# Transposes by halves of the array's rows in a second pass, and value weights cast ahead of the rows in an opening

## The chip, the cores and the metric

The kernel runs on one core of a Trainium2 chip. The metric is the device time of one execution in microseconds (us); smaller is better. TensorE is called PE here (PEld is its weight load), VectorE DVE, ScalarE ACT, GpSimd POOL, and the engine that only issues DMAs SP. SBUF is the memory from which the engines read; PSUM is where PE writes its results.

## The reference

Four residual layers, A, B, A, B, on 2048 rows of 512 numbers, with 32 heads of 16 columns:

```
x = x + A(layernorm(x)); x = x + B(layernorm(x))      # twice
A: q, k, v = x @ wqkv, by heads;  pq = q @ w_phi[h];  pk = k @ w_phi[h]
   phi(p) = [softmax(p), softmax(-p)]                  # 32 features
   o = phi(pq) @ (phi(pk)^T v) / (phi(pq) . sum phi(pk) + 1e-6);  return o @ wo
B: per segment of 512 rows: softmax attention inside it, gated with
   a read of a memory that sums phi(k)^T v over the earlier segments; @ wo
```

Layer A is linear in the rows: a first pass over all rows sums the state phi(pk)^T v, a second pass reads it for each row. These are the linear layers of the change.

## The kernel before, in words

Everything is computed to about fp32 accuracy: each operand of a large product is split into a high part (the fp32 number rounded to a shorter format, "fp32r", by a cast on ACT) and a low part (a subtraction on DVE or POOL), and a product is three products: high by high, high by low, low by high. `mm3` writes these for the four blocks kc of the 512 inner numbers, block by block; with `low_last` it first takes those whose moving rows or columns are high. All PE instructions are issued through `mm` (L177) and `tp` (L181, a transpose: a matmul with the identity as moving operand), and `held` keeps them in the order of the code. All other instructions go through a helper at L155, which keeps the order of the code on each engine; SP issues the DMAs in the order of the code too. In `out<-in` names the second name behind the comma of a PE row is the operand that is loaded into the array.

**Opening** (`LayerA.first`). SP asks for the key weights, the first 512 rows and the value weights. While the rows' layer norm is computed (`moments` to `refine`, `normal`: tags st and x), PE folds w_phi into the key weights. `columns` transposes one tile of 128 normalised rows (four transposes into a PSUM tile g), casts it (ACT: hh) and takes the low part (DVE: hl). Behind the four `columns` come the value weights' casts on ACT (w<-P) and their low parts, by turns on DVE and POOL; then `v_tile` computes the values of the four tiles of rows.

**Second pass** (`LayerA.pass2`), one step i for each of the 16 tiles of 128 rows. A tile's features e (tag P) are exponentials of the query projections tb, 1024 per row; `scale_q` sums them on DVE (es), takes reciprocals (rr) and scales half of them on POOL (P<-P,rr). `transposed` turns them by eight transposes into the PSUM tile lg, which ACT copies to phT (P<-lg). `products` multiplies phT, loaded by 64 columns, with the state KN (32 small products into two PSUM tiles g), and DVE divides (r, U). In the next step `turn` transposes the row of outputs U by four transposes into g; ACT casts it (oh), DVE takes the low part (ol), and `out_proj` multiplies it with the output weights w, whose eight loads (high and low part of each kc by turns) are asked for at the pass's start; DVE adds the residual rows (ot<-g,ot) and SP stores them. The features are turned one step ahead, and scaled two ahead. The pass is woven with layer B's opening by a table of step numbers. The last output tiles (from i = 12) and the transposes of tiles 14 and 15 are handed on to layer B, which takes them in slots chosen by a count of PE work (`work`). The PSUM tiles g have several buffers; lg, mx and my have one each.

Of the kernel before, what the change touches and what calls it, by code (L numbers as in the profile page):

```python
# [7 lines left out]
F32 = mybir.dt.float32  # L8
F32R = mybir.dt.float32r
# [92 lines left out]
def interleave_kernel(ctx, tc, x_in, a_wqkv, a_wphi, a_wo, b_wq, b_wk, b_wv, b_wo, b_beta,  # L102
# [76 lines left out]
    def tp(*a):  # L179
        work[0] += 108  # L180
        return held(nc.tensor.transpose(*a))  # L181

# [252 lines left out]
    def mm3(po, lhs, rhs, kcs=range(NC), low_last=False):  # L435

        terms = [(kc, a, b) for kc in kcs for a, b in ((0, 0), (0, 1), (1, 0))]
        if low_last:
            terms.sort(key=lambda x: x[1])
        for n, (kc, a, b) in enumerate(terms):  # L440
            mm(po, lhsT=lhs(a, kc), rhs=rhs(b, kc), start=(n == 0), stop=(n == len(terms) - 1))
            if n % 3 == 2 and n < len(terms) - 1:
                yield
# [33 lines left out]
    def tok_proj(po, hT, t, w):  # L477
        yield from mm3(po, lambda a, kc: hT[a][:, kc, t * P : (t + 1) * P], lambda b, kc: w[b][:, kc, :])

    def turn(ot):  # L480

        o = [T2("oh", OO, F32R), T2("ol", OO, F32R)]
        pt = PS("g", G)
        for c, block in enumerate(ot):
            tp(pt[:, c * P : (c + 1) * P], block, ident)
        pt, hi, lo = [t[:, 0 : len(ot) * P] for t in (pt, *o)]
        act.copy(hi, pt)
        wait(lambda: dve.tensor_tensor(out=lo, in0=pt, in1=hi.bitcast(F32), op=SUB))
        return o

# [52 lines left out]
    def v_tile(hT, w, vv, tag, order=range(4), pairs=False):  # L543
# [4 lines left out]
        if not pairs:  # L548
            for t in order:
                po = PS(*tag)  # L550
                yield from tok_proj(po, hT, t, w)
                act.copy(v[:, t, 0 : H * VW].rearrange("p (h e) -> p h e", e=VW)[:, :, 0:DH],
                         po.rearrange("p (h e) -> p h e", e=DH))
                yield
            return
# [94 lines left out]
    class LayerA:  # L650
# [4 lines left out]
        def first(self, hT, vv, upcoming):  # L655

            wph = T2("U", UU)[:, 0 : NC * DH].rearrange("p (c f) -> p c f", c=NC)
            act.dma_start(out=ident, in_=c_ident)
            act.dma_start(out=bd, in_=c_bd)
            act.dma_start(out=wph, in_=a_wphi.rearrange("(c h) d f -> (h d) c f", c=NC))  # L660
# [25 lines left out]
            next(kfold)  # L686
            normal(st, 0, xt[0])
# [3 lines left out]
            for t in range(4):  # L691
                columns(hT, t, xt[t])
            upc = upcoming(1)
            next(upc[1])
            for kc in range(NC):
                act.copy(vh[:, kc, :], vraw[kc])
                low(pool if kc % 2 else dve, wv, kc, vraw[kc])
            for kc in range(NC):
                act.copy(kh[:, kc, :], kf[kc])
                low(dve, wk, kc, kf[kc])  # L700
            vt = v_tile(hT, wv, vv, ("g", G))
# [230 lines left out]
        def transposed(self, i):  # L932
# [6 lines left out]
            for half in range(2):  # L939
                for q in range(4):  # L940
                    g = 4 * half + q
                    tp(pt[:, half, q * P : (q + 1) * P], ef[:, g * P : (g + 1) * P], ident)
                if i in (1, 2):
                    act.copy(f[:, 4 * half : 4 * half + 4].rearrange("p g t -> p (g t)"), pt[:, half])
                elif half == 1:
                    act.copy(f.rearrange("p g t -> p (g t)"), pt.rearrange("p h x -> p (h x)"))
# [18 lines left out]
        def pass2(self):  # L965
# [5 lines left out]
            for i in range(NT):  # L971
                soon = [i + 2] if i < NT - 5 else [i + 2, i + 3] if i == NT - 5 else [i + 3]
                soon = [n for n in soon if 2 < n < NT]
                if i > 0:
                    if i <= NT - 4:
                        oT = turn([self.o[:, c * P : (c + 1) * P] for c in range(NC)])
# [4 lines left out]
                    if i >= NT - 4:  # L981
                        yield from transposed(i + 1)
                    yield from self.products(i)
                if 2 < i < NT - 4:
                    yield from transposed(i + 1)
# [11 lines left out]
                if 0 < i <= NT - 4:  # L997
                    steps = out_proj(x, self.xdst, i - 1, oT, self.wo, i == 1)
# [634 lines left out]
```

## Time and profile before

| | |
|---|---|
| median of three runs | 1307.09 us (1305.85 to 1308.08) |
| the profiled execution | 1307.07 us, its span 1305.4 us |
| mean granted clock of PE | 0.999 |
| busy in the span | PE 97%, PEld 76%, DVE 82%, ACT 64%, POOL 58% |
| turning the features (lg<-ident,P) | 256 transposes, 35.9 us busy |
| turning the outputs (g<-ident,U) | 96 transposes, 14.4 us busy |
| reading the state (g<-KN,P) | 1024 products, 37.4 us busy |
| DMA | 196.59 MB in the span, 151 GB/s in the mean |

Busy times of PE overlap: a matmul's row runs from its issue to its end, and the next one starts before that. So the cost of one of a row of equal matmuls is read from start to start, not from its duration. In a timeline row the count behind x tells how many equal instructions follow each other; the time is from the first's start to the last's end. In brackets stands how long the engine was idle before, and which engine's work ended that (the releaser). Idle time of an engine that isn't waited for costs nothing.

### The profile page before, as it was taken

The numbers are of one execution on the slowest core, as the hardware profiler recorded it, in microseconds if no ns is written. First come the engines' busy times: TensorE is split into PE (matmuls) and PEld (weight loads), VectorE is DVE, ScalarE is ACT, GpSimd is POOL, SyncE is SP. The second block draws the span as 40 slices with busy tenths as digits, with TensorE's granted clock in tenths as the row PEclk, the third lists the DMA queues.
The fourth block names the chain that finished last, engine by engine and source line by source line (L and its number), as shares of the span: only waits on it lengthen the run. The fifth ranks groups of instructions, "written<-read, shape, count | busy, mean of one in ns | idle before, by whom it ended". The sixth has DMA issues, their size and how long they took to land.

```text
span 1305.4 us, 41985 instructions
## 1 busy us (share of the span) xinstructions
PE 1266.3 (97%) x16488; PEld 988.1 (76%) x16488; DVE 1073.8 (82%) x3499; ACT 835.9 (64%) x1214; POOL 757.8 (58%) x1124
## 2 busy tenths in 40 slices
PE   7999989999999999999999999999999999999987
PEld 6887868877777777777768887787777777778765
DVE  4776868798998998998867767797899899898995
ACT  5556444648778788777644434455678878877754
POOL 2568855425657768667324346562356766767653
PEclk9999999999999999999999999999999999999999
DMA  6387358545655545545451101855646555554432
GB/s 213 106 314 258 123 175 254 175 125 147 185 164 152 160 126 142 160 134 162 128 174 54 66 34 37 290 176 162 163 127 205 163 141 143 144 142 113 120 84 82
DMA packets 134420, 196.59 MB, mean 151 GB/s; under 512 B 15440, under 2 KB 61648, under 8 KB 133456
## 3 DMA queue, kind: packets, MB, share of 16 engines
q1 hardware_dynamic: 133408, 193.80, 49.1%
q8 instruction: 131, 2.15, 0.7%
q14 instruction: 65, 0.53, 0.1%
q10 hardware_dynamic: 816, 0.11, 0.1%
HBM read 101.05 MB, written 39.85 MB: 108 GB/s over the span
## 4 chain that ended last, share of the span: by engine, by line
PE 77%; DVE 15%; issue 2%; ACT 2%; POOL 2%; DMA 2%; SPq 0%; DVEq 0%; ACTq 0%; POOLq 0%
PE g L177 60%; PE lg L177 6%; PE g L181 4%; PE mx L177 3%; DVE g L155 3%; DVE U L155 2%; PE lg L181 2%; DVE mx L155 2%; DVE my L155 2%; DVE es L155 1%; PE my L177 1%; POOL P L155 1%; DVE mxs L155 1%; ACT P L155 1%; DMA P<-in 1%
## 5 line engine op out<-in xcount | busy, mean ns | idle before, releaser
L155 ACT ACTIVATE P<-lg 128x1024 f32<-128x1024 f32 x316 | 324.1, 1026 | 94.8 <-PE lg L177 75.8
L155 POOL TENSOR_SCALAR_AFFINE_SELECT P<-P 128x256 f32<-128x256 f32 (+1 forms) x448 | 190.0, 442 | 227.4 <-ACT P L155 205.7
L155 DVE CUSTOM_DVE_ANT_0 g<-g,mask 128x128 f32<-128x128 f32 (+3 forms) x392 | 189.4, 538 | 7.0 <-PE g L177 6.7
L155 DVE CUSTOM_DVE_ANT_0 mx<-mx,mask 128x512 f32<-128x512 f32 (+2 forms) x316 | 158.8, 503 | 38.9 <-PE my L177 28.7
L177 PE MATMUL g<-hh,wqk 64*128 64x512 f32 (+1 forms) x960 | 183.2, 393 | 0.7 <-SPq L155 0.4
L177 PE MATMUL g<-w,oh 64*128 64x512 f32 (+2 forms) x848 | 161.8, 380 | 2.6 <-ACT oh L155 2.6
L155 DVE CUSTOM_DVE_ANT_0 my<-my,mask 128x512 f32<-128x512 f32 (+2 forms) x316 | 163.5, 517 | 0.0
L177 PE MATMUL lg<-e,e 64*128 64x512 f32 (+1 forms) x1010 | 145.8, 343 | 7.6 <-ACT P L155 7.5
L177 PE MATMUL g<-P,v 128*32 128x128 f32 (+3 forms) x2064 | 151.7, 433 | 0.2
L177 PE MATMUL g<-w,hh 64*128 64x512 f32 (+1 forms) x672 | 143.5, 395 | 2.4 <-ACT w L155 1.3
L155 DVE DVE_READ_ACCUMULATOR2_ANT mxs<- 128x1 f32 x1024 | 142.9, 140 | 0.0
L177 PEld LDWEIGHTS lg<-e,e 64*128 64x128 f32 x1010 | 92.7, 185 | 51.7 <-ACT P L155 19.7
L177 PEld LDWEIGHTS g<-hh,wqk 64*128 64x128 f32 (+1 forms) x960 | 100.0, 185 | 19.5 <-SPq L155 2.0
L177 PEld LDWEIGHTS g<-P,v 128*32 128x32 f32 x2064 | 65.5, 109 | 60.8 <-issue 53.6
L177 PEld LDWEIGHTS g<-w,oh 64*128 64x128 f32 (+1 forms) x848 | 94.7, 187 | 18.8 <-ACT oh L155 3.5
L155 ACT COPY tb<-g 128x512 f32<-128x512 f32 (+1 forms) x132 | 71.1, 575 | 52.3 <-PE g L177 52.0
L177 PE MATMUL g<-w,ol 64*128 64x512 f32 (+2 forms) x424 | 101.0, 377 | 1.9 <-DVE ol L155 1.9
L177 PE MATMUL g<-hl,wqk 64*128 64x512 f32 (+1 forms) x480 | 102.1, 390 | 0.0
L177 PEld LDWEIGHTS g<-w,hh 64*128 64x128 f32 (+1 forms) x672 | 83.8, 188 | 17.9 <-ACT w L155 1.6
L177 PE MATMUL g<-w,hl 64*128 64x512 f32 (+1 forms) x336 | 89.3, 392 | 0.0
L155 POOL TENSOR_TENSOR ta<-tb,ta 128x512 fp32r<-128x512 f32 x60 | 76.2, 1291 | 14.0 <-ACT ta L155 11.1
L177 PE MATMUL mx<-e,e 63*128 63x256 f32 (+3 forms) x323 | 82.0, 318 | 0.8 <-DVE r L155 0.8
(163 smaller groups left out, 2935.7 us busy)
## 6 DMA issues: line engine op xcount, KB each, us to landing
e<-ta SPq DMA_DIRECT2D x384, 128.0 KB
wqk<-wqk SPq DMA_DIRECT2D x128, 256.0 KB
x<-x SPq DMA_DIRECT2D x48, 256.0 KB
pq<-tb SPq DMA_DIRECT2D x24, 256.0 KB
tb<-pq SPq DMA_DIRECT2D x24, 256.0 KB
x<-xr SPq DMA_DIRECT2D x22, 256.0 KB
xr<-x SPq DMA_DIRECT2D x20, 256.0 KB
x<-in SPq DMA_DIRECT2D x16, 256.0 KB
```

What stands on the lines that cost most here:

```text
L155: i = f(*a, **k)
L177: return held(nc.tensor.matmul(*a, **k))
L181: return held(nc.tensor.transpose(*a))
```

## The change

It has five parts.

1. A transpose of a 128x128 block can be issued as two halves (`tp_halves`): the block's rows 0 to 63 in the array's upper half of rows, rows 64 to 127 in the lower, each with 64 moving columns, each into a PSUM tile of its own.
2. `transposed` uses halves for all its tiles, and copies with one ACT instruction always; before, tiles 1 and 2 were copied in two, half by half.
3. `turn_halves` takes the place of `turn` for i = 1 to 11 of each second pass. It turns into mx and my, casts with two ACT instructions and subtracts with two on DVE.
4. In the second pass, from i = 3, `transposed(i + 1)` stands ahead of `products(i)`. `out_proj` takes `low_last` in the steps 1 and 2 (before: 1 only), and `low_last` now sorts by both parts: all four high by high products, then high rows by low weights, then low rows by high weights.
5. In the opening, the value weights of kc 0 and 1 are cast before the rows are normalised on ACT, those of kc 2 and 3 behind the first tile's cast; DVE takes all four low parts; the first value tile uses `low_last`; and ACT asks for w_phi ahead of the constants bd.

In all 344 of 768 whole transposes of the kernel become 688 halves; ACT has 22 casts more, DVE 22 subtractions more in the second passes and POOL two less in the opening. SP's order is the same.

```diff
@@ -180,6 +180,13 @@
         work[0] += 108
         return held(nc.tensor.transpose(*a))
 
+    def tp_halves(outs, in_):
+
+        work[0] += 60
+        for row, out in zip((0, 64), outs):
+            held(nc.tensor.transpose(out, in_[row : row + 64], ident[row : row + 64, row : row + 64],
+                                     tile_position=(row, 0)))
+
     def dma(out, in_):
         sync.dma_start(out=out.bitcast(F32), in_=in_.bitcast(F32))
 
@@ -436,7 +443,7 @@
 
         terms = [(kc, a, b) for kc in kcs for a, b in ((0, 0), (0, 1), (1, 0))]
         if low_last:
-            terms.sort(key=lambda x: x[1])
+            terms.sort(key=lambda x: x[1:])
         for n, (kc, a, b) in enumerate(terms):
             mm(po, lhsT=lhs(a, kc), rhs=rhs(b, kc), start=(n == 0), stop=(n == len(terms) - 1))
             if n % 3 == 2 and n < len(terms) - 1:
@@ -474,8 +481,9 @@
     def tok_side(po, hT, t, w):
         return po, lambda a, kc: hT[a][:, kc, t * P : (t + 1) * P], lambda b, kc: w[b][:, kc, :]
 
-    def tok_proj(po, hT, t, w):
-        yield from mm3(po, lambda a, kc: hT[a][:, kc, t * P : (t + 1) * P], lambda b, kc: w[b][:, kc, :])
+    def tok_proj(po, hT, t, w, low_last=False):
+        yield from mm3(po, lambda a, kc: hT[a][:, kc, t * P : (t + 1) * P], lambda b, kc: w[b][:, kc, :],
+                       low_last=low_last)
 
     def turn(ot):
 
@@ -487,6 +495,23 @@
         act.copy(hi, pt)
         wait(lambda: dve.tensor_tensor(out=lo, in0=pt, in1=hi.bitcast(F32), op=SUB))
         return o
+
+    def turn_halves(o):
+
+        hi, lo = T2("oh", OO, F32R), T2("ol", OO, F32R)
+        pts = [PS(t, 1)[:, 0 : NC * 64] for t in ("mx", "my")]
+        for c in range(NC):
+            tp_halves([pt[:, c * 64 : (c + 1) * 64] for pt in pts], o[:, c * P : (c + 1) * P])
+        views = [[t.rearrange("p (c r x) -> p r c x", c=NC, r=2)[:, r] for t in (hi, lo)]
+                 + [pts[r].rearrange("p (c x) -> p c x", c=NC)] for r in range(2)]
+        for h, _, pt in views:
+            act.copy(h, pt)
+
+        def low():
+            for h, l, pt in views:
+                dve.tensor_tensor(out=l, in0=pt, in1=h.bitcast(F32), op=SUB)
+        wait(low)
+        return hi, lo
 
     turns = [0]
 
@@ -540,7 +565,7 @@
         dve.tensor_tensor(out=t, in0=p[:, :, :, 0:DH], in1=rb, op=MUL)
         eng.tensor_tensor(out=out, in0=out, in1=t, op=ADD)
 
-    def v_tile(hT, w, vv, tag, order=range(4), pairs=False):
+    def v_tile(hT, w, vv, tag, order=range(4), pairs=False, low_last=None):
         v = sp.tile([P, 4, VROW], F32, tag="v", bufs=2, name=nm("v"))
         vv[:] = [v]
         pool.memset(v[:, :, 0 : H * VW].rearrange("p t (h e) -> p t h e", e=VW)[:, :, :, DH : DH + 1], 1.0)
@@ -548,7 +573,7 @@
         if not pairs:
             for t in order:
                 po = PS(*tag)
-                yield from tok_proj(po, hT, t, w)
+                yield from tok_proj(po, hT, t, w, t == low_last)
                 act.copy(v[:, t, 0 : H * VW].rearrange("p (h e) -> p h e", e=VW)[:, :, 0:DH],
                          po.rearrange("p (h e) -> p h e", e=DH))
                 yield
@@ -656,8 +681,8 @@
 
             wph = T2("U", UU)[:, 0 : NC * DH].rearrange("p (c f) -> p c f", c=NC)
             act.dma_start(out=ident, in_=c_ident)
+            act.dma_start(out=wph, in_=a_wphi.rearrange("(c h) d f -> (h d) c f", c=NC))
             act.dma_start(out=bd, in_=c_bd)
-            act.dma_start(out=wph, in_=a_wphi.rearrange("(c h) d f -> (h d) c f", c=NC))
             nc.scalar.preload_act_table_set("natural_log_exp_and_others")
             kraw = fetch(a_wqkv[:, D : 2 * D])
             xt = rows_of(self.xsrc, SEGS[0])
@@ -684,21 +709,26 @@
             root(st)
             refine(st, dve)
             next(kfold)
+            for kc in (0, 1):
+                act.copy(vh[:, kc, :], vraw[kc])
             normal(st, 0, xt[0])
             for t in (1, 3):
                 dve.tensor_scalar(xt[t], xt[t], st[:, t, 2:3], st[:, t, 3:4], op0=MUL, op1=ADD)
             normal(st, 2, xt[2])
-            for t in range(4):
+            for kc in (0, 1):
+                low(dve, wv, kc, vraw[kc])
+            columns(hT, 0, xt[0])
+            for kc in (2, 3):
+                act.copy(vh[:, kc, :], vraw[kc])
+                low(dve, wv, kc, vraw[kc])
+            for t in range(1, 4):
                 columns(hT, t, xt[t])
             upc = upcoming(1)
             next(upc[1])
             for kc in range(NC):
-                act.copy(vh[:, kc, :], vraw[kc])
-                low(pool if kc % 2 else dve, wv, kc, vraw[kc])
-            for kc in range(NC):
                 act.copy(kh[:, kc, :], kf[kc])
                 low(dve, wk, kc, kf[kc])
-            vt = v_tile(hT, wv, vv, ("g", G))
+            vt = v_tile(hT, wv, vv, ("g", G), low_last=0)
             for t in range(4):
                 for _ in range(4):
                     next(vt)
@@ -937,13 +967,10 @@
             f = self.phT[i] = T2("P4", NP4, shape=(P, 8, P))
             pt = PS("lg", 1, (P, 2, 512))
             for half in range(2):
-                for q in range(4):
-                    g = 4 * half + q
-                    tp(pt[:, half, q * P : (q + 1) * P], ef[:, g * P : (g + 1) * P], ident)
-                if i in (1, 2):
-                    act.copy(f[:, 4 * half : 4 * half + 4].rearrange("p g t -> p (g t)"), pt[:, half])
-                elif half == 1:
-                    act.copy(f.rearrange("p g t -> p (g t)"), pt.rearrange("p h x -> p (h x)"))
+                for g in range(4 * half, 4 * half + 4):
+                    tp_halves([pt[:, r, g * 64 : (g + 1) * 64] for r in range(2)], ef[:, g * P : (g + 1) * P])
+                if half == 1:
+                    act.copy(f.rearrange("p g (r t) -> p r g t", r=2), pt.rearrange("p r (g t) -> p r g t", g=8))
                 yield
 
         def products(self, i):
@@ -973,16 +1000,17 @@
                 soon = [n for n in soon if 2 < n < NT]
                 if i > 0:
                     if i <= NT - 4:
-                        oT = turn([self.o[:, c * P : (c + 1) * P] for c in range(NC)])
+                        if i < NT - 4:
+                            oT = turn_halves(self.o)
+                        else:
+                            oT = turn([self.o[:, c * P : (c + 1) * P] for c in range(NC)])
                         yield
                     for n in soon if i != 1 else ():
                         exp(self.e[n])
                     self.o = T2("ot", OT) if NT - 4 <= i else T2("U", UU)
-                    if i >= NT - 4:
+                    if i > 2:
                         yield from transposed(i + 1)
                     yield from self.products(i)
-                if 2 < i < NT - 4:
-                    yield from transposed(i + 1)
                 for n in [i + 3] if i < NT - 6 else [i + 3, i + 4] if i == NT - 6 else [i + 4]:
                     if 3 < n < NT:
                         self.e[n] = differences(*self.raw.pop(n))
@@ -995,7 +1023,7 @@
                 else:
                     self.rest.append(self.o)
                 if 0 < i <= NT - 4:
-                    steps = out_proj(x, self.xdst, i - 1, oT, self.wo, i == 1)
+                    steps = out_proj(x, self.xdst, i - 1, oT, self.wo, i < 3)
                     if i < 3:
                         for _ in range(2):
                             next(steps)
```

On PE, in layer A's second pass at i = 3, as the rows stand before (x counts equal rows; lg is the turned features of tile 4, g_2533 and g_2545 the products of tile 3 with the state, g_2583 the output product of tile 2):

```order
L181 MATMUL g_2524<-ident,U_2456 128x128 x4
L177 MATMUL g_2533<-KN_2277,P_375_2501 64x68 x8
L177 MATMUL g_2545<-KN_2277,P_375_2501 64x68 x8
L181 MATMUL lg_2560<-ident,P_351_2399 128x128 x8
L177 MATMUL g_2583<-w_2266,oh_2522 128x512
L177 MATMUL g_2583<-w_2267,oh_2522 128x512
```

and after, where the mx and my rows go on by turns, four of each:

```order
L187 MATMUL mx_2568<-ident,U_2492 128x64
L187 MATMUL my_2569<-ident,U_2492 128x64
...
L187 MATMUL lg_2585<-ident,P_352_2421 128x64 x16
L177 MATMUL g_2605<-KN_2277,P_377_2537 64x68 x8
L177 MATMUL g_2617<-KN_2277,P_377_2537 64x68 x8
L177 MATMUL g_2642<-w_2266,oh_2566 128x512
L177 MATMUL g_2642<-w_2267,oh_2566 128x512
```

The features of the next tile are turned before the products of this one, by 16 halves instead of eight transposes.

On PE, the output product of i = 1, before (w_2266 are the high weights, w_2267 the low ones; one row per product until the x4):

```order
L177 MATMUL g_2406<-w_2266,oh_2360 128x512
L177 MATMUL g_2406<-w_2267,oh_2360 128x512
...
L181 MATMUL lg_2414<-ident,P_320_2197 128x128 x8
```

and after:

```order
L177 MATMUL g_2428<-w_2266,oh_2375 128x512 x4
L177 MATMUL g_2428<-w_2267,oh_2375 128x512 x2
L187 MATMUL lg_2436<-ident,P_320_2197 128x64 x16
L177 MATMUL g_2428<-w_2267,oh_2375 128x512 x2
L177 MATMUL g_2428<-w_2266,ol_2376 128x512 x4
```

Before, high and low weights take turns three times ahead of the transposes, that is, the blocks kc 0 to 2; after, the high weights of all four blocks stand first.

On ACT, in the opening before (st: the rows' means and deviations, x: rows, hh: high parts of the turned rows, w_158: high parts of the value weights, two blocks to a row):

```order
L155 ACTIVATE st_155<-st_155 128x4 x2
L155 ACTIVATE x_139<-x_139,st_155 128x512
L155 ACTIVATE x_143<-x_143,st_155 128x512
L155 CAST hh_156<-g_243 128x4x128
L155 CAST hh_156<-g_250 128x4x128
L155 CAST hh_156<-g_257 128x4x128
L155 CAST hh_156<-g_264 128x4x128
L155 CAST w_158<-P_8_147 128x512 x2
L155 CAST w_158<-P_9_149 128x512 x2
```

and after:

```order
L155 ACTIVATE st_155<-st_155 128x4 x2
L155 CAST w_158<-P_8_147 128x512 x2
L155 ACTIVATE x_139<-x_139,st_155 128x512
L155 ACTIVATE x_143<-x_143,st_155 128x512
L155 CAST hh_156<-g_247 128x4x128
L155 CAST w_158<-P_9_149 128x512 x2
L155 CAST hh_156<-g_258 128x4x128
L155 CAST hh_156<-g_265 128x4x128
L155 CAST hh_156<-g_272 128x4x128
```

The two casts of the first blocks stand between st and the rows, the other two behind the first hh.

## The prediction

> **What bounds the kernel now.** I read the page's busy times and its chain first, then the timeline of the two stages that the change touches, then the groups of the instructions that it replaces.
>
> ```profile
> span 1305.4 us, 41985 instructions
> PE 1266.3 (97%) x16488; PEld 988.1 (76%) x16488; DVE 1073.8 (82%) x3499; ACT 835.9 (64%) x1214; POOL 757.8 (58%) x1124
> PE 77%; DVE 15%; issue 2%; ACT 2%; POOL 2%; DMA 2%; SPq 0%; DVEq 0%; ACTq 0%; POOLq 0%
> ```
>
> PE is busy 97% of the span and carries 77% of the chain that ended last. So PE time that is saved passes on to the end, unless PE only waits longer for something else, and a PE stall that is removed passes on too. The profiled execution took 1307.07 us, 1.7 us more than its span and 0.02 us under the median of the runs shown (1307.09); I make the sum against 1307.07.
>
> The first stage touched is the opening (timeline: start, length, engine, operation, and in brackets the idle time before it with its releaser):
>
> ```profile
> 12.46 1.52 ACT L155 ACTIVATE x<-x,st 128x512 f32<-128x512 f32 x2 [1.25 <-DVE st L155]
> 13.33 1.97 PE L181 MATMUL g<-ident,x 128*128 128x128 f32 x16 [1.08 <-ACT x L155]
> 14.03 2.05 ACT L155 CAST hh<-g 128x512 fp32r<-128x512 f32 x4
> 14.64 2.48 DVE L155 TENSOR_TENSOR hl<-g,hh 128x512 fp32r<-128x512 f32 x4 [1.18 <-ACT hh L155]
> 15.94 2.21 ACT L155 CAST w<-P 128x512 fp32r<-128x512 f32 x4
> 16.64 0.49 PE L177 MATMUL g<-w,hh 128*128 128x512 f32 x1 [1.34 <-ACT w L155]
> 17.78 0.50 PE L177 MATMUL g<-w,hh 128*128 128x512 f32 x1 [0.65 <-DVE w L155]
> 18.92 0.80 PE L177 MATMUL g<-w,hh 128*128 128x512 f32 x1 [0.17 <-POOL w L155]
> 22.30 0.63 PE L177 MATMUL g<-w,hh 128*128 128x512 f32 x2
> 25.04 1.91 PE L181 MATMUL g<-ident,P 128*128 128x128 f32 x16
> ```
>
> The value product of tile 0 starts at 16.64, when ACT, done with the rows' casts, has cast the first value weights. It then waits for the weights' low parts, and ends where tile 1 starts, at 22.30: 5.66 us, against 2.74 for tile 1 (22.30 to 25.04). The waits after the start explain only 0.82 of this. The rest is the clock, as a table by stretch shows (PE, PEld, DVE, ACT, POOL busy, granted clock, DMA share, GB/s):
>
> ```profile
> 0.00:11.40 11.40, 6.43 (x42) 6.43 (x43) 3.49 (x10) 4.04 (x7) 1.67 (x8) 1.00 0.84 291
> 20.00:22.00 2.00, 2.00 (x6) 1.60 (x5) 1.35 (x4) 1.56 (x3) 0.88 (x3) 0.50 0.85 323
> ```
>
> From about 18.7 to 22.1 the granted clock is 0.50. The first row also tells that 3.3 MB have landed by 11.4 us, as much as the key weights, the rows and the value weights together (3 x 1.05 MB).
>
> The second stage is layer A's second pass, here one steady iteration with the links of its chain as they stand where nothing else delays them:
>
> ```profile
> 179.15 1.17 PE L177 MATMUL g<-KN,P 128*64 128x68 f32 x32
> 179.89 0.26 DVE L155 RECIPROCAL r<-g 128x16 f32<-128x16 f32 x1 [3.30 <-PE g L177]
> 181.15 1.21 DVE L155 TENSOR_REDUCE es<-P 128x64 f32<-128x1024 f32 x1
> ...
> 196.25 1.09 PE L181 MATMUL lg<-ident,P 128*128 128x128 f32 x8
> 197.73 1.21 DVE L155 TENSOR_REDUCE es<-P 128x64 f32<-128x1024 f32 x1
> 198.97 0.35 DVE L155 RECIPROCAL rr<-es 128x32 f32<-128x32 f32 x1
> 199.70 1.06 POOL L155 TENSOR_TENSOR P<-P,rr 128x512 f32<-128x512 f32 x1 [1.17 <-DVE rr L155]
> 201.61 1.09 PE L181 MATMUL lg<-ident,P 128*128 128x128 f32 x8
> ...
> 222.44 1.05 POOL L155 TENSOR_TENSOR P<-P,rr 128x512 f32<-128x512 f32 x1 [1.74 <-DVE rr L155]
> 223.55 1.09 PE L181 MATMUL lg<-ident,P 128*128 128x128 f32 x8 [0.35 <-POOL P L155]
> ...
> 246.18 1.09 PE L181 MATMUL lg<-ident,P 128*128 128x128 f32 x8
> 248.30 2.12 PE L177 MATMUL g<-hh,wqk 128*128 128x512 f32 x8
> ```
>
> At 200.76 POOL has ended the scaling of the next features, and their transposes start at 201.61: 0.85 us of slack. At 223.55 the slack is gone and PE waits 0.35 for POOL. The second pass is therefore close to a balance of PE and the chain KN product, r, es, rr, POOL, transposes.
>
> **The pair of halves.** 344 of the whole transposes become pairs of 64-row halves. A whole one costs 110 ns: 16 took 1.97 us at 13.33 and 8 took 1.09 at 196.25, so 8 more take 0.88. No row shows a half. The nearest rows:
>
> ```profile
> L181 PE MATMUL lg<-ident,P 128*128 128x128 f32 x256 | 35.9, 280 | 3.9 <-ACT P L155 2.8 <-POOL P L155 1.0
> L177 PE MATMUL g<-KN,P 128*64 128x68 f32 x1024 | 37.4, 226 | 0.0
> L177 PEld LDWEIGHTS g<-KN,P 128*64 128x64 f32 x1024 | 32.8, 137 | 5.2 <-issue 4.0 <-DVE ot L155 0.3 <-DVE mxs L155 0.3
> L181 PEld LDWEIGHTS lg<-ident,P 128*128 128x128 f32 x256 | 27.7, 140 | 10.8 <-ACT P L155 4.2 <-POOL P L155 2.7 <-issue 2.4
> L177 PEld LDWEIGHTS lg<-phibd,e 128*128 128x128 f32 x32 | 4.0, 195 | 0.1
> 302.20 0.28 PE L177 MATMUL mx<-e,e 63*128 63x256 f32 x1
> 302.24 0.28 PE L177 MATMUL my<-e,e 63*128 63x256 f32 x1
> 302.32 0.27 PE L177 MATMUL mx<-e,e 63*128 63x256 f32 x1
> ```
>
> Two KN products side by side, each with 68 moving columns of fp32, take 61 ns: 32 in 1.17 us less one duration of 0.226, over 31, is 30.5 each. A pair of halves moves 64 columns. Its load is the doubt. The load of a whole transpose (140 ns) is as short as that of a 64-column product (137), not as that of a 128-column product (195), so it isn't what holds a whole transpose at 110. Products in opposite row halves do overlap: mx and my start 0.04 apart, and the next pair 0.12 after the first. I take 60 ns for a pair, nearest to the KN row, with 55 (half of a whole one) and 110 (halves in series) as the ends. 344 x 50 ns would be 17.2 us, if all of it lay on the path.
>
> [...]
>
> **Opening.** ACT's four value casts (0.55 each) leave the place ahead of the first product; two go into the 1.25 us in which ACT waits for st, two into its wait for the transposes. The weights have landed by then (3.3 MB row). DVE takes all four low parts, 0.62 each as the hl (2.48 for four): two in its 1.18 us of waiting, two after the first hl. POOL loses its two; nothing waits for POOL there. The third and fourth hh casts come no later than the product needs them, since tile 0 needs one tile of rows only. The hi terms come first, so the low parts aren't asked for until four products later. Tile 0 can start about 15.4, when PE has done the last row transposes, and at the full clock ends 2.74 later, at 18.1 instead of 22.30: 4.1 us after 0.1 for queueing. Ends: 1.2 (only the start moves) and 4.4.
>
> **Second pass, steady part (i from 3).** The transposes now stand ahead of the KN products, so the chain no longer has them beside it; it has them in it. One turn: 8 pairs and a change of mode, 0.48 + 0.13 (248.30 less 246.18 is 2.12, against 0.88 + 0.98 for the products, so 0.13 for each of two changes); KN to r 0.74; r to es 1.26; es to rr 1.24; rr to POOL 0.73; POOL to transposes 1.11. Sum 5.69. From the transposes at 196.25 to those at 246.18 before has nine such periods in 49.93, 5.55 each; after, nine in 51.2. PE's own work falls from 5.36 (196.25 to 201.61) by 12 pairs x 50 ns less two changes of mode, to about 5.0, so PE now waits some 0.7 per iteration, and the waiting is for POOL. The end, from 246.18 to 248.30, falls by 0.4. Together +0.9 per layer. The 11 more casts and subtractions of each pass (22 of either engine in all) lie on ACT and DVE beside this; the casts become halves, and what they add is the fixed part, 0.1 to 0.2 each, on the way to the output product, which has 0.7 of PE's waiting to spare.
>
> **Second pass, front (i = 1, 2).**
>
> ```profile
> 178.56 0.66 PE L181 MATMUL lg<-ident,P 128*128 128x128 f32 x4 [0.75 <-ACT P L155]
> 186.14 0.66 PE L181 MATMUL lg<-ident,P 128*128 128x128 f32 x4 [0.68 <-ACT P L155]
> 191.33 0.50 PE L177 MATMUL g<-w,ol 128*128 128x512 f32 x1 [0.95 <-DVE ol L155]
> 175.11 4.44 SPq L155 DMA_DIRECT2D w<-awo  x8
> ...
> 175.10:183.60 8.50, 7.75 (x97) 6.37 (x96) 4.99 (x13) 4.10 (x6) 1.12 (x2) 1.00 0.75 221
> ```
>
> The three stalls (2.38) go, and 24 pairs save 1.2. What is late next: the first output product asks for the fourth block's hi weights at its fourth product instead of its seventh or later. The eight weight loads are issued from 175.11, seven of them are 1.84 MB, and in the 8.5 us up to 183.60 221 GB/s make 1.88 MB. So the product, which could start about 182, stands until about 183.9, some 1.9 us. DVE's chain through es and rr to the next transposes, whose links don't shrink, keeps another 0.7 by my addition of its rows. Left: -1.0 per layer. Ends 0 and -3.6. So the second pass is worth -0.1 per layer, -0.2 in all.
>
> **Tiles 14 and 15.** Their 16 transposes per layer are taken in layer B, between products of 64 rows, on a PE that doesn't wait: 32 x 50 ns, -1.6.
>
> **Sum:** -4.1 - 0.2 - 1.6 = -5.9; with half a microsecond kept back, since each iteration's DVE queue also takes the second subtraction ahead of es, -5.4: 1301.7 us, 0.41% faster.
>
> **Rivals.**
> A. The chain doesn't bind, because es or the scaling moves up with the transposes. Then the pairs are worth their PE time: 312 x 50 ns less about 60 changes of mode of 0.13, some -7.5, and -4.1 - 7.5 - 1.6 = -13.2: 1293.9. For it: the chain had 0.85 of slack. Against: its links above don't shrink, and 223.55 shows them binding already. Chance 0.08.
> B. The halves run in series (110 ns or more a pair). Each turn of the chain then takes 0.40 more, 3.6 for nine; the end and the front lose their 1.6; both layers 10.4; tiles 14 and 15 give nothing: -5.4 + 10.4 + 1.6 = +6.6: 1313.7, slower. It decides from about 0.082 a pair. For it: one set of 128 columns per half is loaded twice as often. Against: the overlap at 302.20. Chance 0.13, with pairs between the ends.
> C. The opening gives only its earlier start: the clock falls in spite of it, or tile 0 waits for hl and low parts in turn. -1.2 instead of -4.1: 1304.6, within 0.2%. For it: PE's longest wait before the clock fell is only 1.34 us, so what makes it fall isn't idleness alone. Against: after the change PE has no such wait. [...] Chance 0.18, with the second pass's longer wait for weights, which ends there too.
>
> **How the numbers follow.** The forecast has 0.61, A 0.08, C 0.18, B 0.13. About 0.2% (2.6 us) is what a measurement of this kernel can tell from no change. Faster by more: the forecast and A, 0.69, of which I give 0.02 to same; slower 0.13; same 0.20. The range runs from 1296.5, between the forecast and A, to 1307.5, past C and into B's small end.
>
> **What would show it.** The value product's start near 15.4 and a clock of 1.00 from 16 to 24 (opening). Half transposes with 16 in about 0.7 us rather than 1.0 (pair). PE idle ahead of the lg halves, released by POOL P, 8 to 14 us over both passes, and a period of 5.7 (chain). A wait on DMA for w in the first output product, 1 to 2.5 us per layer (front). It would be wrong if 16 half transposes took 0.95 us, if the period were under 5.3, or if the clock still fell to 0.50 near 18.

## The result and the profile after

The changed kernel takes 1315.99 us in the median (1315.06 to 1319.74) against 1306.47 us: a ratio of 1.0079, 95% interval 1.0054 to 1.0103. A second, longer timing gave 1.0048 (1.0030 to 1.0065). It is slower, and lies above the forecast range; the forecast was faster.

The page after, with busy times and the chain:

```profile
span 1318.0 us, 42698 instructions
PE 1265.2 (96%) x16832; PEld 978.4 (74%) x16832; DVE 1078.5 (82%) x3523; ACT 836.6 (63%) x1232; POOL 753.7 (57%) x1122
PE 69%; DVE 17%; DMA 4%; POOL 3%; SPq 2%; issue 2%; ACT 2%; DVEq 0%; POOLq 0%; ACTq 0%
```

PE's busy time hardly changes (1266.3 before), its share of the chain falls from 77% to 69%; DMA, DVE and SP's queue take about two points each of the rest, POOL one. The profiled execution was the longest of its four, 1319.74 us.

The opening, in the timeline of the profile after (columns as before):

```profile
15.50 2.12 PE L177 MATMUL g<-w,hh 128*128 128x512 f32 x8
17.46 1.08 PE L177 MATMUL g<-w,hl 128*128 128x512 f32 x4
18.38 0.62 PE L177 MATMUL g<-w,hh 128*128 128x512 f32 x2
21.10 1.91 PE L181 MATMUL g<-ident,P 128*128 128x128 f32 x16
```

The first value product starts at 15.50 instead of 16.64, both tiles run at full speed, and the transposes of P follow at 21.10 instead of 25.04. The front of the first second pass:

```profile
170.51 0.71 PE L187 MATMUL lg<-ident,P 64*128 64x64 f32 x16
...
177.57 1.38 PE L177 MATMUL g<-w,oh 128*128 128x512 f32 x3
181.66 1.65 PE L177 MATMUL g<-w,oh 128*128 128x512 f32 x3 [2.71 <-DMA w<-awo]
183.24 1.11 PE L187 MATMUL lg<-ident,P 64*128 64x64 f32 x16
...
190.93 0.71 PE L187 MATMUL lg<-ident,P 64*128 64x64 f32 x16 [0.52 <-POOL P L155]
194.60 0.71 PE L187 MATMUL lg<-ident,P 64*128 64x64 f32 x16 [0.96 <-POOL P L155]
200.32 0.71 PE L187 MATMUL lg<-ident,P 64*128 64x64 f32 x16 [0.53 <-POOL P L155]
206.03 0.71 PE L187 MATMUL lg<-ident,P 64*128 64x64 f32 x16 [0.51 <-POOL P L155]
```

After three products PE waits 2.71 us for the fourth block of the high weights. The 16 halves behind it take 1.11 us instead of 0.71: the clock has fallen. The table by stretch (granted clock third from the end) shows it, and the steady step:

```profile
178.00:180.00 2.00, 0.81 (x3) 0.19 (x1) 1.93 (x7) 0.00 (x0) 2.00 (x3) 1.00 0.98 299
180.00:181.00 1.00, 0.00 (x0) 0.00 (x0) 0.31 (x1) 0.00 (x0) 0.44 (x1) 0.80 1.01 368
183.00:184.00 1.00, 1.00 (x15) 0.76 (x16) 0.00 (x0) 0.00 (x0) 0.95 (x1) 0.50 1.05 393
186.00:187.00 1.00, 1.00 (x3) 0.39 (x2) 0.00 (x0) 0.37 (x1) 0.00 (x0) 0.50 0.08 28
188.00:189.00 1.00, 1.00 (x29) 0.93 (x26) 1.00 (x1) 1.00 (x3) 0.00 (x0) 1.00 0.19 76
206.03:211.75 5.72, 5.21 (x68) 4.11 (x68) 4.39 (x11) 2.51 (x5) 3.19 (x5) 1.00 0.91 280
```

The clock falls at 180.6, is 0.50 until about 187.4, and then the steady period is 5.72 us with 0.5 of it PE waiting for POOL's P. From the first transposes (lg) to those of tile 4 the front takes 24.1 us (170.51 to 194.60), against 21.4 before (174.89 to 196.25).

For all profiles I cut the span at five marks: the opening's g<-ident,P; the first lg of each second pass; the first of the eight g<-hh,wqk products behind each pass. The times between them, and from the last to the end, are, in us (front: the part of a second pass up to the lg of tile 4):

| kernel | opening | rest of pass 1 | second pass 1 (front) | layer B 1 | second pass 2 (front) | layer B 2 | span |
|---|---|---|---|---|---|---|---|
| before | 25.04 | 149.9 | 73.4 (21.4) | 561.3 | 73.7 (21.4) | 422.0 | 1305.4 |
| before, again | 24.05 | 150.5 | 73.8 (21.4) | 562.7 | 74.4 (22.2) | 421.7 | 1307.1 |
| after | 21.10 | 149.4 | 78.1 (24.1) | 566.6 | 77.9 (23.6) | 424.9 | 1318.0 |
| after, again | 21.12 | 149.3 | 77.1 (23.0) | 564.8 | 78.5 (24.4) | 422.8 | 1313.6 |
| after, third | 20.97 | 149.6 | 76.8 (22.8) | 564.5 | 77.4 (23.4) | 423.3 | 1312.5 |
| opening only | 21.35 | 150.5 | 73.4 (21.4) | 562.5 | 73.7 (21.4) | 422.1 | 1303.5 |
| halves only | 25.18 | 149.4 | 71.9 (20.6) | 563.2 | 73.3 (22.1) | 421.9 | 1304.8 |
| both orders back | 21.03 | 149.8 | 74.0 (21.2) | 562.2 | 73.1 (21.8) | 423.1 | 1303.2 |
| whole 14, 15 | 21.34 | 149.7 | 72.8 (21.8) | 563.3 | 71.9 (21.0) | 422.4 | 1301.5 |
| products first | 21.04 | 149.8 | 75.8 (24.9) | 564.3 | 71.2 (20.7) | 423.4 | 1305.6 |
| old sort | 21.18 | 149.9 | 74.4 (20.4) | 563.6 | 75.3 (21.0) | 423.1 | 1307.5 |
| high first, reorder | 21.18 | 149.5 | 73.6 (19.6) | 562.7 | 74.8 (20.8) | 424.6 | 1306.4 |
| high first | 21.07 | 150.2 | 70.4 (19.9) | 562.5 | 72.9 (22.3) | 423.6 | 1300.6 |
| reorder only | 24.79 | 149.3 | 77.8 (20.6) | 565.9 | 78.1 (21.0) | 421.5 | 1317.4 |
| reorder only, again | 25.18 | 150.1 | 77.8 (20.6) | 562.3 | 77.8 (20.6) | 422.1 | 1315.3 |
| halves for lg only | 21.14 | 150.1 | 70.9 (20.1) | 562.3 | 70.4 (19.4) | 423.3 | 1298.1 |
| the same, again | 21.07 | 149.6 | 70.3 (19.2) | 562.1 | 71.1 (19.6) | 421.6 | 1295.8 |

### The profile page after: what moved, and what is told of

The parts are those of the page before. It is cut to its first block, busy times and chain, and to the rows that moved or that the text cites. A ratio compares the mean times of both kernels' runs of the same rounds, so it can differ in the third digit from the quotient of the medians.

```text
span 1318.0 us, 42698 instructions
## 1 busy us (share of the span) xinstructions
PE 1265.2 (96%) x16832; PEld 978.4 (74%) x16832; DVE 1078.5 (82%) x3523; ACT 836.6 (63%) x1232; POOL 753.7 (57%) x1122
## 4 chain that ended last, share of the span: by engine, by line
PE 69%; DVE 17%; DMA 4%; POOL 3%; SPq 2%; issue 2%; ACT 2%; DVEq 0%; POOLq 0%; ACTq 0%
PE g L177 54%; PE lg L177 6%; PE g L181 3%; PE mx L177 3%; DVE es L155 3%; DVE U L155 2%; POOL P L155 2%; SPq L155 2%; DVE g L155 2%; DVE mx L155 2%; PE my L177 1%; DVE my L155 1%; DMA w<-awo 1%; DMA wqk<-wqk 1%; DMA e<-ta 1%
## 5 line engine op out<-in xcount | busy, mean ns | idle before, releaser
L155 ACT ACTIVATE P<-lg 128x1024 f32<-128x1024 f32 x316 | 324.3, 1026 | 98.0 <-PE lg L177 77.1
L177 PE MATMUL g<-w,oh 64*128 64x512 f32 (+2 forms) x848 | 164.8, 384 | 8.2 <-DMA w<-awo 5.1
L177 PEld LDWEIGHTS g<-hh,wqk 64*128 64x128 f32 (+1 forms) x960 | 100.6, 185 | 23.6 <-SPq L155 4.8
L155 ACT COPY tb<-g 128x512 f32<-128x512 f32 (+1 forms) x132 | 71.2, 576 | 53.9 <-PE g L177 53.6
```

What stands on the lines that cost most here:

```text
L155: i = f(*a, **k)
L177: return held(nc.tensor.matmul(*a, **k))
```

## The experiments

Ratios are to the kernel before, timed beside each, with the 95% interval.

**The change again**, unaltered.

> The changed kernel once more, unaltered. Its first profile (1319.7 us, the slowest of its four runs) lost 3.3 us more than before to waits of PE for SP in layer B. If these are chance, a second profile shows a span near 1314 and waits for SP under 1.5 us; if they belong to the change, they are there again at 3 to 4 us.

1.0048 (1.0030 to 1.0065), span 1313.6, which is near the 1314 of chance. PE's waits for SP came to 2.7 us over the whole span, between the two cases I had named (under 1.5, or 3 to 4): the extreme of the first profile was in part chance, and the stages of this profile are used below.

**The opening alone.**

```diff
 # kernel before, with first(), v_tile and tok_proj of the change
-            terms.sort(key=lambda x: x[1])
+            terms.sort(key=lambda x: x[1:] if low_last == 'new' else x[1])
```

> The kernel before with only the change of the opening (its casts, low parts and the order of the first value tile). The opening gained 3.9 us in every profile. If the 1 to 5 us that layer B lost in all changed profiles come from its start being shifted in time (its transfers then meet others), 0 to -2 us against before remain here; if they come from the halves or the count of PE work, layer B keeps its length and the run is 3.9 us faster than before, -0.3%.

0.9961 (0.9949 to 0.9973). The opening's 3.7 us reach the end, and layer B keeps its length (562.5 and 422.1): starting earlier costs it nothing.

**The halves alone** (both orders and the opening of before).

> The changed kernel with the orders and the opening of before: only the halves are left. Both orders taken back gave -0.33% with the opening. If the parts add, this is within 0.2% of before: second passes -0.1 in all, layer B +2. If the opening shifts layer B badly, this is faster, 1303 or less.

0.9999 (0.9986 to 1.0013): no gain, no loss.

**Both orders taken back** (halves and opening left), and the same with **whole transposes for tiles 14 and 15**.

```diff
-                    if i > 2:
+                    if i >= NT - 4:
                         yield from transposed(i + 1)
                     yield from self.products(i)
+                if 2 < i < NT - 4:
+                    yield from transposed(i + 1)
-            terms.sort(key=lambda x: x[1:])
+            terms.sort(key=lambda x: x[1] if low_last == 'old' else x[1:])
-                    ... out_proj(x, self.xdst, i - 1, oT, self.wo, i < 3)
+                    ... out_proj(x, self.xdst, i - 1, oT, self.wo, 'old' if i == 1 else False)
```

> The changed kernel with both orders of before: the halves and the opening are left. Theories F and S together: opening -4, front -2 per layer, steady -6 per layer, tiles 14 and 15 -1.6, so about 1286 to 1290 us. If the sums don't add, because a wait in layer B takes it back, 1295 to 1300.

> Both orders and whole transposes for tiles 14 and 15, which are taken in layer B; the rest as changed. My prediction's own term: 1.6 us slower than with both orders taken back. Rival: the step of 1.2 us in each layer B that all four changed profiles show (at about 445 and 1075 us of the kernel before) belongs to these halves or to their smaller count of PE work; then it is gone and the run is about 1 us faster.

0.9967 (0.9958 to 0.9977) and 0.9970 (0.9955 to 0.9984): the parts add, but the second pass gains far less than I expected, and tiles 14 and 15 give no difference that these intervals can tell (my 1.6 us are 0.12%, about their width). The traces tell more. From the start of the instruction ahead of these transposes to that of the one behind them, the three places of a layer take 2.1 us with halves and 3.1 with whole transposes, so the halves do save 1.0 there. But by the same exponentials on ACT only 0.1 of it is left 54 us into the first layer B, and the step near 445 us (a wait of PE put down to issue, 1.2 us) then puts the halves behind. That step is gone with whole transposes there, as the rival had it; waits for issue of 0.63 and 0.53 stand at the end of that layer instead, and the time is the same. Why the halves give so little in the second pass stands in three views: the steady step, of before and then of both orders back,

```profile
201.61:206.97 5.36, 5.36 (x61) 4.53 (x57) 4.23 (x10) 2.56 (x4) 3.13 (x3) 1.00 0.77 231
```

```profile
197.14:202.28 5.14, 5.14 (x73) 4.12 (x70) 4.75 (x11) 2.63 (x5) 3.14 (x3) 1.00 0.96 304
...
222.00:223.00 1.00, 1.00 (x4) 0.79 (x3) 1.00 (x2) 0.97 (x2) 1.00 (x2) 0.50 0.97 342
```

and POOL and PE (timeline) of the latter:

```profile
216.03 1.06 POOL L155 TENSOR_TENSOR P<-tb,mmq 128x512 f32<-128x512 f32 x1 [3.38 <-DMA tb<-pq]
218.29 1.06 POOL L155 TENSOR_TENSOR P<-P,rr 128x512 f32<-128x512 f32 x1 [0.19 <-DVE rr L155]
219.41 0.71 PE L187 MATMUL lg<-ident,P 64*128 64x64 f32 x16 [1.50 <-POOL P L155]
```

PE is busy throughout both steps, and a step with halves is only 0.22 us shorter, not the 0.34 of my sum. Only the first three of the nine periods are as short as this; the last six add up to 33.9 and 34.2 us in the two passes of before, and with halves in the order of before to 33.2 to 34.0, apart from the one pass with a slow stretch in it. Where a load of tb comes late, POOL is late and PE waits 1.50; the clock then falls to 0.50 for 3.4 us, which costs 1.7 more.

**Products first** (only the order of transposes and products taken back) and **old sort** (only the order of the output products taken back; the two halves of the diff above).

> The changed kernel with the features turned behind the products from step 3, as before. Theory F: the steady period falls from 5.72 to about 5.0 us, nine times in each layer, but the front's wait and slow clock stay: 1316 - 12 = 1304. Rival S: the same 1304. Rival H (halves don't save PE time in this place): period 5.36 as before, 1310.

> The changed kernel with the output products of the second pass in the order of before (high rows first in step 1 only, block by block). Theory F (front: the output product asks too early for the last high weights; the wait of 2.7 and 2.4 us is followed by a halved clock): no wait for the output weights, clock 1.00 from 174 to 200, and about 4.5 us per layer back, 1307 us. Rival S (the steady part is the cause, each iteration's transposes waiting for POOL): 1314 or more, since the steady period stays 5.72 us.

1.0004 (0.9990 to 1.0017) and 1.0009 (0.9999 to 1.0019): each order is worth about 0.4% (5 to 6 us), and together 0.8%. So neither theory alone holds; the front and the steady part cost about the same. With products first a step is 5.14 us and PE busy throughout, and in the first front the wait for w (0.43 and 3.21 us) and the slow clock are still there (24.9). In the second front PE waits for w for 0.81 and 0.83 us, the clock stays at 1.00, and the front takes 20.7, less than before. With the old sort the period stays 5.72, and the clock stays at 1.00 in both fronts; but the waits for w aren't gone, as theory F had it: they are 1.42 us in the first front and 2.03, in three pieces, in the second.

**The reorder alone**, on the kernel before with whole transposes.

```diff
-                    if i >= NT - 4:
+                    if i > 2:
                         yield from transposed(i + 1)
                     yield from self.products(i)
-                if 2 < i < NT - 4:
-                    yield from transposed(i + 1)
```

> The kernel before, with nothing changed but that from step 3 the features are turned (by whole transposes) ahead of the products. If the loss of the steady part is the chain that now has the transposes in it, its period is 0.64 us (halves) to 0.84 us (whole) from transposes to products more: 5.72 + 0.20 = 5.9 us, against 5.55 in the mean before; nine of them in each of two passes make +6 us, 1313, +0.5%, with no clock below 1.00 there. If the reorder only costs together with the halves (their changes of mode), the period stays near 5.5 and the run within 0.2%.

1.0072 (1.0059 to 1.0085), more than the 0.5% that I expected; a step of it:

```profile
200.80 1.09 PE L181 MATMUL lg<-ident,P 128*128 128x128 f32 x8 [0.49 <-POOL P L155]
206.90 1.09 PE L181 MATMUL lg<-ident,P 128*128 128x128 f32 x8 [0.49 <-POOL P L155]
```

The period is 6.10 us, and PE waits for POOL in every step. The order costs this by itself; the halves only shorten the transposes in the chain.

**High weights first.** The output weights are asked for as hi 0 to 3, then lo 0 to 3; once with the reorder of the change, once with products first.

```diff
-            for kc in range(NC):
-                for t, k in zip((hi, lo), kept[key]):
+            for t, k in zip((hi, lo), kept[key]):      # for the key "awo" only
+                for kc in range(NC):
                     dma(t[:, kc, :], k[:, kc, :])
```

> The changed kernel as it is, but with the four high blocks of the output weights asked for ahead of the four low ones. Front alone: the wait for w of 2.7 and 2.4 us goes, and with it the halved clock of 3.4 to 6.8 us behind it: -3 to -5 us per layer, 1307 to 1309 us, while the period stays 5.72.

> The order of products and transposes as before, the new order of the output products kept, and the output weights asked for in another order: the four high blocks first, then the four low ones. If the front was lost to the late landing of the fourth high block, the wait for w and the halved clock of the front are gone (high blocks landed about 6 us after their issue), and the front takes about 18.5 us from the first transposes to those of tile 4, against 21.4 before and 24.9 with the wait: 1299 to 1302 us.

1.0008 (0.9998 to 1.0017) and 0.9965 (0.9952 to 0.9977). With the reorder, the wait for w in the first front falls to 0.36 us:

```profile
179.62 0.49 PE L177 MATMUL g<-w,oh 128*128 128x512 f32 x1 [0.36 <-DMA w<-awo]
```

The clock doesn't fall in either front, and they take 19.6 and 20.8 us instead of 23 to 24: the late high block was the cause of the front's loss. A wait of 1.27 us is left in the second front, for the last low block. The second run missed its forecast in the fronts: 19.9 and 22.3 us, where I had 18.5. In its profile the clock fell for 3.4 us in each of them, once behind a wait of 1.73 us for w and once behind one of 1.65 us put down to issue, ahead of the pass. Why it isn't faster than both orders back stays open: that kernel's profile has a slow stretch of 3.4 us in each pass too, and over their timed runs the mean granted clock is 0.999 for high first and 0.998 for both orders back.

**Halves for the features only**: as high first, but the outputs are turned whole again.

```diff
-                        if i < NT - 4:
+                        if False:
                             oT = turn_halves(self.o)
```

> As the run hi_first (opening, order of before, high weights first), but the outputs U are turned whole again, with one cast and one subtraction: halves are left for the features only. In the trace a step's saving is 0.20 us at the features and 0.04 at the outputs, so the period should be 5.18 instead of 5.14, and ACT and DVE have 11 instructions less in each pass: the same time as hi_first within 0.2%, 1303.

0.9932 (0.9920 to 0.9944), about 0.3% below high first, where I had expected no difference: it beats both kernels. Its step is what the rows had said,

```profile
196.50:201.69 5.19, 5.19 (x70) 4.29 (x66) 4.61 (x10) 2.57 (x4) 3.14 (x3) 1.00 0.86 264
201.69:206.87 5.18, 5.18 (x67) 4.28 (x65) 4.29 (x10) 2.56 (x4) 3.26 (x5) 1.00 0.88 287
```

so the halves of the outputs saved PE 0.05 us a step. Without them the clock fell in no second pass of its two profiles. The wait for issue near 445 us is gone, though tiles 14 and 15 are still turned by halves, and one of 1.3 us stands at the end of that layer B instead. So these halves alone don't bring it; that it goes with where an instruction stands in PE's stream is only a guess.

**Layer B's length**: the kernel before once more, the change a third time, the reorder and the halves for lg a second time, one profile each.

> The kernel before, for a second profile: how much its layer B varies by itself. Its first profile took 561.3 us from the first pass's end of reading to the next layer's first transposes, the changed kernel's two took 566.6 and 564.8, the others 562.2 to 564.3. If this one is under 562, the halves cost layer B 1 to 3 us; if it is above 563, they cost it nothing that can be told from chance.

> The changed kernel, a third profile. If layer B's longer time belongs to the change: 564.5 to 567 us for the first layer B again. If it is chance: anywhere from 561 to 567.

> The reorder alone, a second profile. If the reorder in the second pass makes layer B longer: 565 to 566 again. If chance: it may be 561 to 563 as in the kernel before.

> Halves at the features alone, order of before, high weights first, a second profile. If layer B's time goes with the reorder: 562 to 563 again. If chance: it may be 564 or more.

562.7, 564.5, 562.3 and 562.1 us. The first lies between the two cases that I had named, and tells nothing by itself. The reorder isn't the cause: its first 565.9 held a clock that had fallen for 3.4 us at 656 us, and its second is 562.3. The changed kernel is at 564.5 or more three times, before and the reorder at 561.3 to 562.7 where the clock held.

## Why the prediction was wrong, point by point

I take the changed kernel's second profile, whose time (1315.3) is nearest to the median, against the first of before: +8.2 us. My sum had -5.4.

- **Opening: right.** -3.9 against -4.1; alone 0.9961. The chance C gave it, that the clock would fall anyway, didn't come true in any profile with the change. In the second profile of before the clock held too and the opening still took 24.05, so 2.9 of the gain are the order and about 1 is the clock. The prediction put all of the lost time behind the 0.82 us of waits down to the clock, about 2.1 us; at a clock of 1.00 tile 0 still took 4.57 us in that profile (5.66 in the first), so only 1.1 was the clock's. The size came out right even so, since the sum took tile 0 at the speed of tile 1, whatever had slowed it.
- **The pair of halves: right in isolation, mis-sized in place.** 16 halves take 0.71 us, so 15 halves from start to start with a duration of 0.23 for the last leave 0.064 a pair; rival B is refuted. The prediction's doubt was the load: in the profile after, the loads of 16 halves take 0.57 us in all (at 200.31). But eight pairs with their change of mode replaced 0.84 by 0.64 us, and four replaced 0.53 by 0.39 and cost 0.10 more behind the output product: 0.24 a step, not the 0.34 of "12 pairs less two changes of mode". The step that failed is that sum, in its first term. In the order of before the halves bring two changes of mode more per step, as the sum had: from whole products to the outputs' halves (0.09 us) and from the features' halves to whole products (0.13). But from first start to last, eight pairs are only 0.33 us shorter than eight whole transposes (0.49 against 0.82) and four pairs 0.09 (0.24 against 0.33): 0.42 where 12 pairs at 50 ns are 0.60.
- **The steady part: right in kind, too small.** I forecast a chain with a period of 5.69 and PE idle for POOL; it is 5.72, and PE idles 0.5 instead of 0.7. That isn't luck: in the profile after, every link from KN to r, es, rr, POOL and the transposes (0.74, 1.26, 1.24, 0.73, 1.11) is as in the sum, and only the halves take 0.64 instead of 0.61. The two half casts of a step take 0.37 and 0.38 us there, a whole one 0.59 in the profile before: 0.17 more in all, inside the 0.1 to 0.2 of the prediction. The loss is 1.8 to 2.0 per layer instead of 0.9, mostly since the last two periods are 5.9 and 6.0 (my nine equal ones had 5.69).
- **The front: wrong, and the largest miss.** -1.0 forecast, +1.7 and +3.0 measured, in the first profile +2.7 and +2.2. Two terms failed. The product that waits for the seventh weight load started 10.9 us after the first issue (170.74 to 181.66), not 8.8: I had divided the seven loads by the whole queue's 221 GB/s, as if the rows and other weights in the queue moved for nothing. At 254 GB/s these 10.9 us moved 2.8 MB, of which the seven loads are 1.84. And I priced a wait as its own length: behind 2.7 us of waiting the clock fell to half for 3.4 or 6.8 us, 1.7 to 3.4 more. A hint was in the prediction, where the clock fell behind waits of 1.34 and 0.65 us; I used it for the opening and not here. Such waits don't always bring it: the second profile of before has the same ones (1.34, 0.63) and kept its clock; the section on the hardware below says what sets them apart. In the first profile after the clock fell 1.7 us into the wait, behind a stretch of 3.41 us in which PE was busy for 1.62.
- **Tiles 14 and 15, and layer B: wrong.** -1.6 forecast; taking them back changed nothing that can be told (0.9967 and 0.9970). The halves save 1.0 us of PE per layer there, more than the 0.8 of the sum, so the price of a pair was not the error. What failed is "on a PE that doesn't wait": PE waits in layer B too, and the gain is gone before its end. Layer B grew by 3.5 and 0.8 us. PE's waits for SP in the first layer B, in the first profiles of before and after (us in all, times, longest):

```profile
PE g L177 <- SPq L155: 0.6, 2, 0.4
```

```profile
PE g L177 <- SPq L155: 3.9, 7, 1.3
```

  In the change's second profile they are 2.7 us; over the ten profiles with the outputs' halves they are 1.5 to 3.9 (2.4 in the mean), over the seven without 0.3 to 1.7 (0.9). Executions differ by 1 to 2 us there by themselves. Over both layers B the ten profiles with the outputs' halves have 987.1 us in the mean, the seven without them 984.7. Why isn't settled: that the halves shift PE's waits for issue and for SP is what the traces suggest, and no run changes it alone.
- **Rivals.** A (the chain doesn't bind) was wrong: it bound in every step. The other sign came, but not by B's mechanism; that a wait for weights could turn the front's sign I had put with C as a small loss.

## What to carry to other kernels

Before asking for data earlier in an order, count when the last piece lands with everything else that is in the queue (here 10.9 us after the first issue, not the 8.8 of the seven loads alone), and price a wait that would leave PE busy for less than about half of some 3.4 us with a stretch of half clock behind it, as something that may happen: in these profiles each of the ten stretches at full clock under 48% had one behind it, 3.4 or 6.8 us long. An edit that moves work ahead of the product that feeds the next step puts it into the step's chain: add the chain up before counting the engine's busy time. Halve transposes where there are many in a row (the features' eight saved 0.20 us a step here); between other modes four of them saved next to nothing (0.04). And take a second profile of the kernel before ahead of explaining a slow stretch in the first.

## What the runs showed of the hardware that was not expected

**When the clock falls.** In each profile, any two recorded changes of the granted clock lie a whole number of times 3.413 us apart (in the first profile after, 189 times from the fall at 180.6 to the one at 825.7). So the span can be cut into stretches of 3.41 us that end where a change can come. For the opening of before, which has the same waits in both of its profiles, and for the front after, this gives (columns as in the table by stretch; first two stretches of before's second profile, whose changes of clock lie only at the span's end, then one of its first, then one of after):

```profile
13.33:16.74 3.41, 2.00 (x17) 1.77 (x17) 2.23 (x5) 3.36 (x8) 0.00 (x0) 1.00 0.67 220
16.74:20.16 3.42, 2.60 (x9) 1.63 (x10) 3.35 (x4) 2.00 (x5) 2.91 (x2) 1.00 0.90 244
...
15.23:18.64 3.41, 1.42 (x5) 0.67 (x4) 3.41 (x6) 3.40 (x7) 1.46 (x1) 1.00 0.96 303
...
177.19:180.60 3.41, 1.62 (x19) 0.79 (x15) 3.05 (x9) 0.13 (x1) 3.09 (x3) 1.00 0.98 320
```

In the second profile the waits are shared out between two stretches, with PE busy for 2.00 and 2.60 us, and the clock holds; in the first they lie in one, with 1.42, and it falls at that stretch's end. The 17 profiles together bear this out for the most part. Leaving out the last 8 us of each span, there are 18 falls, and 15 come behind a stretch in which PE was busy for 20 to 55%. From 8 us into the span on, each of the ten stretches at full clock with less than 48% was followed by a fall; between 48 and 56% some were and some weren't. So whether a wait of 1 to 2 us costs a slow stretch is partly chance: the old sort waited 1.42 us for w in its first front and had 1.99 us busy in that stretch, and kept its clock. Three falls came behind 72 or 73%, all in fronts of kernels with the outputs' halves; these stay unexplained.

**The outputs' halves and the clock.** The clock fell inside a second pass in eight of the ten profiles of kernels with the outputs' halves, each time to 0.50 and for 3.4 or 6.8 us, and in none of the seven without them. This isn't shown to be the halves' doing. The kernels without them have shorter waits in their fronts (0.75, 0.68 and 0.95 us in before), and over the timed runs the mean granted clock is lowest in the kernels whose profile has the longest waits of PE for w (in brackets, in us over the span): 0.9960 for the change (5.9 in its second profile) and 0.9961 for products first (5.3), then 0.9978 for both orders back (2.2), 0.9988 for the old sort (3.4) and 0.9989 for both kernels with high weights first (1.8 with the reorder, 2.1 without), all with the outputs' halves, against 0.9993 for the opening alone (none of 0.4 or more in its fronts) and 0.9995 for the halves of the features only (one of that length, 0.73). Among the middle ones the order isn't that of the waits.

**Pairs of halves.** Halves in opposite row groups ran side by side: in the profile after, those into mx and my start together (176.08), and 16 halves take 0.71 us, 0.064 a pair from start to start, where eight whole transposes took 1.09 in the profile before, 0.11 each.
